# One tile of four banks for the row maxima of windowed attention, scales in a weight tile's corner, and later copies to DRAM

## The chip, the cores and the metric

The kernel runs on one core of a Trainium2 chip. The core has five engines that run side by side and wait for each other by semaphores: TensorE (PE; its weight loads are shown apart as PEld), VectorE (DVE), ScalarE (ACT), GpSimd (POOL) and SyncE (SP), whose queue issues the DMAs here. Matmul results land in PSUM, a memory of eight banks of 512 fp32 columns on 128 partitions, from which VectorE and ScalarE read. The metric is the device time of one execution in microseconds (us).

## What is computed

The input x has 2048 tokens of 512 channels. Cut to what matters:

```python
xn = layernorm(x)
q, k, v = split(xn @ wqkv)                      # 32 heads of 16 channels
scores = q @ k.T * 16 ** -0.5                   # per head
scores = where(0 <= query - key < 256, scores, -1e9)
s = concat(softmax(scores) @ v) @ wo
h = gelu(layernorm(xn) @ w1 + b1)               # 1792 hidden channels
g = silu(h @ w2 + b2)
out = x + s * g
```

## The kernel before

**Split numbers.** fp32 operands go through TensorE as a high and a low part (fp32r), so that a product is three passes: high by high, high by low, low by high.

**Stages.** A start loads x, normalises it and writes its transpose, `big` (the name `xnT` in the profile), with both parts. Then comes attention, then the MLP with its projection `w2` into accumulators `acc`, the product with `wo`, and the gate. Weights and parts of `big` are parked in DRAM and fetched back later (`stage_in`, `keep_xt`, `fetch`).

**Attention by slots.** Heads go in eight groups n of four (a head is one of the places p, a of a pair of pairs). q and k of a group lie in `slots[n % 2]` (tile `qk`); row 3 of each 32 rows of q holds the negated row maximum, which comes in through DRAM (`mT_d`) by way of `max_rows`. There are 128 slots t: slot t stands for block `t % 16` of 128 queries of group `t // 16`. The loop runs over pairs u, of an even slot 2u and an odd slot 2u + 1; pairs with `u % 8 == 0` begin a group of heads. In each pair:

- `prob_part(u, 0..2)` computes transposed scores into the PSUM tile `stb`, ScalarE takes the exponential into `pt`, GpSimd cuts the triangles.
- `pv_part(u)` multiplies `pt` with v into `otb`, which is columns 256 to 511 of the second bank of the PSUM tile `zo`; ScalarE copies it to `oraw` (two buffers) and a DMA takes it to DRAM.
- The row maxima of block t + 12 (`LEAD`) are computed, 12 slots ahead of use.
- Fill units from lists keyed by slot (`fills`) keep TensorE busy: the projections to q, k and v and the first hidden columns, in the banks `fb`. A unit is two matmuls of 64 rows side by side. `plan` and `ends` hold other steps by slot, DMA issues among them; `late` moves some of VectorE's operations to the end of the odd slot.

All instructions of an engine keep the order in which the code issues them.

**The maxima.** A block of 128 queries sees three blocks of 128 keys: the one two before it, partly, the one before it, wholly, and its own, partly. The first and the own are exclusive by position, so `COPY_PREDICATED` with a triangle mask merges the first into the own in PSUM. Two matmuls (a = 1, 0) use the upper and the lower 64 rows of the array and run together: a pair.

- `max_ends` (tile `xy`, two banks): two pairs of 256 columns, first and own keys. Then the merge, and a maximum over 512 elements.
- `max_middle` (columns 0 to 255 of the two banks of `zo`): two pairs of 128 columns and a maximum over 512 elements into a second half of `mt`.
- `max_rows`, every fourth block, joins both halves with a minimum (they are negated) before it sends the rows off.

In an even slot the order is ends, middle, then the operations of VectorE: merge, maximum of the middle, maximum of the ends. In an odd slot the middle comes right behind `prob_part(u, 2)`, then two thirds of the slot's fill units (rounded up), then the ends, the rest of the units, `prob_part(u + 1, 0)` and `pv_part(u)`.

**The scales.** The second layernorm is a scale per token. Its row for the first 512 tokens is spread over the partitions by a DMA (`fetch_scales(0, ...)`): once at slot 80 into a tile with the tag `wa`, which `g_first` takes over at the end of attention, and once more into a tile `scales` after attention. The hidden column tile f = 1 (`first_h(1, False)`) is copied unscaled and multiplied by GpSimd when the second copy is there.

**Copies to DRAM.** `keep_xt` sends twelve pieces of `big` of 512 KB to `xt_d`, behind slots 25, 29, ... 69. `stage_in` copies weights from slot 23 on, one in four slots.

Of the kernel before, what the change touches and what calls it, by code (L numbers as in the profile page):

```python
# [9 lines left out]
F32 = mybir.dt.float32  # L10
# [3 lines left out]
ALU = mybir.AluOpType  # L14
AX = mybir.AxisListType
# [34 lines left out]
def mixer_kernel(ctx, tc, x, wqk, wv, wo, w1, b1, w2, b2, out):  # L50
# [127 lines left out]
    mT_d = dram.tile([NQ, NCH, 32, P], F32, name="mT_d")  # L178


    xy = psum.tile([P, 2, 512], F32, name="xy")
    zo = psum.tile([P, 2, 512], F32, name="zo")
    otb = zo[:, 1, 256:512]
    mids = zo[:, :, 0:256].rearrange("q a (p k) -> q a p k", p=2)
    ends_of = xy.rearrange("q a (p e k) -> q a p e k", p=2, e=2)
    psf = attn.enter_context(tc.tile_pool(name="psf", bufs=1, space=PSUM))
    fb = [psf.tile([P, 512], F32, name=f"fb{i}") for i in range(2)]
    early = ExitStack()
# [33 lines left out]
    nc.gpsimd.memset(mhalf, -0.5)  # L222
    make_identity(nc, ident)
    clear_rows(0, ((nc.vector, 0, 1536), (nc.scalar, 4096, 7168), (nc.gpsimd, 1536, 4096), (nc.gpsimd, 7168, 8192)))
    scales = None
    mask = upper.bitcast(I32).unsqueeze(1).unsqueeze(1).to_broadcast([P, 2, 2, P])
    b1s = const.tile([P, NF], F32, name="b1s")
    sv = small.tile([P, 32], F32, tag="sv", name="sv", bufs=1)
# [258 lines left out]
    def pair_h(f):  # L487

        def mm(ps, k, r, **flags):
            kt, (a, b) = k // 3, PASSES[k % 3]  # L490
            return nc.tensor.matmul(ps, w1_part(a, f)[r, P * kt: P * (kt + 1)], mlp["yy"][b][kt][r], **flags)

        def finish(ps, t, copy):
            raw = t2.tile([P, 512], F32, tag="t2", name=f"hr_{f}")
            if 5 < f < 12:
                copy(raw, ps)
            else:
                nc.vector.tensor_mul(raw, ps, scales)
            if f < 4:
                soon[f] = raw  # L500
            else:
                behind(t, nc.sync.dma_start, h_d[f - 6], raw)
        return 3 * KT, mm, finish
# [51 lines left out]
        r = slice(64 * a, 64 * a + 64)  # L555
        nc.tensor.matmul(out, slot[r, 0, p, P * qb: P * (qb + 1)], keys(slot[r, 1, p]), start=True, stop=True)

    def max_places(n, qb):

        if (n, qb // 4) not in mts:  # L560
            mts[n, qb // 4] = small.tile([P, 2, 2, 2, 4], F32, tag="mt", name=f"mt_{n}_{qb}", bufs=2)
        return (mts[n, qb // 4][:, i, :, :, qb % 4] for i in range(2))

    def max_ends(n, qb):

        mt, _ = max_places(n, qb)
        for p in range(2):
            for a in (1, 0):
                if qb < 2:
                    max_scores(ends_of[:, a, p, 0], n, qb, a, p, lambda row: row[:, P * qb: P * qb + 1].to_broadcast([64, P]))  # L570
                    max_scores(ends_of[:, a, p, 1], n, qb, a, p, lambda row: row[:, P * qb: P * (qb + 1)])
                else:
                    max_scores(ends_of[:, a, p], n, qb, a, p,
                               lambda row: row.rearrange("d (b k) -> d b k", k=P)[:, qb - 2: qb + 1: 2])
        own = ends_of[:, :, :, 1]
        outs["max"] = nc.vector.copy_predicated(own, mask, ends_of[:, :, :, 0]),
        return lambda: nc.vector.tensor_reduce(out=mt, in_=own, axis=AX.X, op=ALU.max, negate=True)

    def max_middle(n, qb):

        if qb == 0:
            return
        _, mu = max_places(n, qb)
        for p in range(2):
            for a in (1, 0):
                max_scores(mids[:, a, p], n, qb, a, p, lambda row: row[:, P * (qb - 1): P * qb])
        nc.vector.tensor_reduce(out=mu, in_=mids, axis=AX.X, op=ALU.max, negate=True)

    def max_block(n, qb):

        rest = max_ends(n, qb)
        max_middle(n, qb)
        rest()

    def max_rows(n, c, t):

        both = mts.pop((n, c))
        mt = both[:, 0]
        mh = small.tile([P, 2, 2, 2, 4], F32R, tag="mh", name=f"mh_{n}_{c}", bufs=2)
        pairs = slice(0 if c else 1, 4)  # L600
        nc.vector.tensor_tensor(mt[:, :, :, pairs], mt[:, :, :, pairs], both[:, 1, :, :, pairs], op=ALU.min)
        eng = nc.gpsimd if t >= -1 else nc.vector
        eng.tensor_copy(mh[:, :, 0], mt)
        eng.tensor_tensor(mh[:, :, 1], mt, mh[:, :, 0].bitcast(F32), op=ALU.subtract)
        mT = small.tile([P, 32], F32, tag="mT", name=f"mT_{n}_{c}", bufs=2)

        for fn, args in todo_dve:
            fn(*args)
        todo_dve.clear()
        nc.vector.transpose(mT, mh.rearrange("p a l i b -> p (a l i b)").bitcast(F32))  # L610
        rows = mT_d[n, c]

        def bring_in():
            nc.sync.dma_start(slots[n % 2][3:P:32, 0, :, 512 * c: 512 * (c + 1)].bitcast(F32),
                              rows.rearrange("(h p b) t -> h p (b t)", h=4, p=2))
        (at if t < 0 else behind)(t + (t < 0), nc.sync.dma_start, rows.rearrange("r (i t) -> i r t", i=4), mT)
        behind(t + 1 + (t < 0), bring_in)
# [67 lines left out]
    def scale_parts():  # L685

        def variance():
            nc.gpsimd.memset(sv, 0.0)
            for i in range(4 * NCH):
                if i in squared:  # L690
                    nc.gpsimd.tensor_scalar(sv[:, i: i + 1], sums[:, i, 1:2], 1.0 / D, None, op0=ALU.mult)
            i = 0
            while i < 4 * NCH:
                k = i
                while k < 4 * NCH and k not in squared:
                    k += 1
                if k > i:
                    nc.gpsimd.tensor_copy(sv[:, i: k], mvs[:, i: k, 1])
                i = k + 1

        def ratio():
            for _ in range(2):
                nc.gpsimd.tensor_tensor(sv[:, 0: 4 * NCH], sv[:, 0: 4 * NCH], rss[:, 0: 4 * NCH], op=ALU.mult)
            nc.gpsimd.tensor_scalar(sv[:, 0: 4 * NCH], sv[:, 0: 4 * NCH], EPS, None, op0=ALU.add)

        def power(c):
            at = sv[:, 4 * c: 4 * c + 4]
            nc.gpsimd.tensor_tensor(at, at, mhalf, op=ALU.pow)
        return variance, ratio, power

    def fetch_scales(c, dst):

# [163 lines left out]
    at(72, nc.vector.transpose, svT, sv)  # L876
    for b in range(4):
        behind(73 + b, nc.sync.dma_start, s_d[:, b], svT[32 * b: 32 * b + 4 * NCH])
    def open_scales():
        nonlocal scales  # L880
        scales = bigp.tile([P, 512], F32, tag="wa", name="scales_0")
        fetch_scales(0, scales)
    behind(80, open_scales)
    for k in range(KT * (NCH - 1)):
        behind(25 + 4 * k, keep_xt, 1 + k // KT, k % KT)
    by_vector = nc.vector.tensor_copy
    on_pool = nc.gpsimd
    for k, (kind, j) in enumerate([*(("w1", j) for j in range(7)), *(("w2", j) for j in range(7)), ("wo", 0), ("wo", 1)]):
# [6 lines left out]
    for f, t, lo_at, lo_by in ((6, 90, 93, nc.vector), (7, 95, 96, nc.vector), (8, 96, 98, on_pool), (9, 99, 101, nc.vector),  # L895
# [4 lines left out]
        at(t, settle, "w1", f, nc.scalar.copy)  # L900
        at(lo_at, settle, "w1", f, None, lo_by)
    at(113, open_w2, 0)
    for f in range(W2_FIRST):
        at(114 + f // 2, fetch, "w2", f)
        at(121 + f, settle, "w2", f, by_vector, nc.vector)
# [8 lines left out]
            split(t[:, 2 * k], t[:, 2 * k + 1], soon[f], by_vector)  # L914
            ready[f] = t[:, 2 * k], t[:, 2 * k + 1]

    def first_h(f, scaled=True):

        for k in range(3 * KT):
            hidden_mm(fb[f], f, k)  # L920
        ready[f] = t2.tile([P, 512], F32, tag="t2", name=f"hf_{f}")
        if scaled:
            nc.vector.tensor_mul(ready[f], fb[f], scales)
        else:
            nc.vector.tensor_copy(ready[f], fb[f])

    ready = {}
    fills[16 * NQ, 0] = [(first_h, (0,))]
# [27 lines left out]

    end = 16 * NQ

    def own_max(part, m):
        return part(m // 16, m % 16) if m < end else lambda: None  # L960

    def own_rows(m, t):
        if 0 <= m < end and m % 4 == 3:
# [24 lines left out]
    for u in range(end // 2):  # L988
        t = 2 * u
        prob_part(u, 1)  # L990
        rest = own_max(max_ends, t + LEAD)
        own_max(max_middle, t + LEAD)
        rest()
        calm[0] = t < end - LEAD
        planned(t)
        fill_in(t, 0)
# [1 line left out]
        ended(t)  # L998
        t += 1
        prob_part(u, 2)  # L1000
        own_max(max_middle, t + LEAD)
        todo = fills.get((t, 0), [])
        n = sum(fn.__name__ == "unit" for fn, _ in todo)
        now[:] = t, 0
        run(delayed.pop((t, 0), ()))
        n -= n if u % 8 == 0 else n // 3
        for fn, args in todo[:n]:
            fn(*args)
        planned(t)
        fill_in(t, 1)  # L1010
        own_max(max_ends, t + LEAD)()
        calm[0] = False
        own_rows(t + LEAD, t)
        for fn, args in todo_dve:
# [15 lines left out]
    for k in sorted(delayed):  # L1030
        run(delayed[k])
    nc.sync.on = False
    first_h(1, False)


    open_w2(1)
# [7 lines left out]
    cp = ctx.enter_context(tc.tile_pool(name="cp", bufs=1))  # L1044
    b2s = cp.tile([P, 512], F32, name="b2s")
    scales = cp.tile([P, 512], F32, name="scales")
    fetch_scales(0, scales)
    wos = cp.tile([P, 2, 4, 512], F32R, name="wos")
    for f in range(W2_FIRST, NF):
        fetch("w2", f)  # L1050
# [4 lines left out]
                              oT_d[2 * g: 2 * g + 2, :, DH].rearrange("i j (c t) -> (i j) c t", c=NCH))  # L1055
        return den

    nc.gpsimd.tensor_tensor(ready[1], ready[1], scales, op=ALU.mult)
    for f in range(6, NF, 2):
        t = gp.tile([P, 2, 512], F32, tag="ohl", name=f"hr_{f}", bufs=4)  # L1060
        nc.sync.dma_start(t, h_d[f - 6: f - 4].rearrange("f p t -> p f t"))
        ready.update({f: t[:, 0], f + 1: t[:, 1]})
        for k in range(2 if f < 12 else 0):
            nc.gpsimd.tensor_tensor(t[:, k], t[:, k], scales, op=ALU.mult)
        if f == 8:
            den = fetch_sums()
    nc.sync.dma_start(b2s, bass.AP(tensor=b2.tensor, offset=b2.offset, ap=[[0, P], [1, 512]]))

    for g in range(4):
# [442 lines left out]
```

## Time and profile before

| | |
|---|---|
| time, median of 3 runs (lowest to highest) | 739.04 us (738.04 to 739.04) |
| time of the profiled execution | 737.41 us |
| its span, first to last instruction | 735.7 us |
| granted TensorE clock, mean over the span | 0.998 |
| attention's main loop (first pv group to the end of the last) | from 67.8 to about 417 us |
| mean DMA rate over the span | 145 GB/s |

Rows of the profile name an instruction by engine, operation, and output<-inputs under the program's tile names: `zo<-pt,vt` is `pv_part`, `zo<-qk` is `max_middle`, `xy<-qk` is `max_ends`, `stb<-qk` is `prob_part`, `fb<-...` are fill units, and `mt<-xy` and `mt<-zo` are the maxima. All have the line L42, that of the helper which keeps the order. In the timeline a row is a run of like instructions: start, length, and in brackets the idle time of the engine before it and what ended it. Matmuls are pipelined: a run's length holds the drain of its last one, while the next run has begun.

### The profile page before, as it was taken

What the parts mean: (1) busy time and instruction counts of PE and PEld (TensorE: products, weight loads), DVE (VectorE), ACT (ScalarE), POOL (GpSimd) and SP (SyncE); (2) the same over time, 40 slices, a digit from 0 to 9 for tenths busy, and PEclk for the clock granted to TensorE, in tenths of its full rate; (3) what the DMA queues carried; (4) which work ended last, traced back from release to release, by engine and by line L of the source; (5) the groups of instructions that cost most, each with busy time, mean ns of one, the idle gap of its engine ahead of it and who ended that gap; (6) DMA issues with size and microseconds to landing.
All of it is one profiled execution on the core that took longest, in us unless ns stands there. A gap on an engine that the chain in (4) does not pass through costs nothing.

```text
span 735.7 us, 17763 instructions
## 1 busy us (share of the span) xinstructions
PE 717.6 (98%) x6944; PEld 580.7 (79%) x6944; DVE 507.7 (69%) x863; ACT 411.7 (56%) x628; POOL 298.9 (41%) x500
## 2 busy tenths in 40 slices
PE   8999999998899999999999999999999999999997
PEld 7998777776678887777777787888888888888886
DVE  7886787876677667778884667536687855667823
ACT  7767777766577566777877726232353734541001
POOL 7344666755468554676777550113202000001102
PEclk9999999999999999999999999999999999999999
DMA  8325455767787733667824465547213322163701
GB/s 294 79 48 126 96 137 142 201 179 205 200 236 202 207 113 97 160 157 192 222 75 153 154 219 147 195 130 238 91 58 104 104 79 86 63 186 113 253 16 58
DMA packets 66275, 106.95 MB, mean 145 GB/s; under 512 B 12624, under 2 KB 21072, under 8 KB 66192
## 3 DMA queue, kind: packets, MB, share of 16 engines
q1 hardware_dynamic: 66192, 105.82, 50.5%
q8 instruction: 55, 0.90, 0.5%
q14 instruction: 28, 0.23, 0.1%
HBM read 54.80 MB, written 33.82 MB: 120 GB/s over the span
## 4 chain that ended last, share of the span: by engine, by line
PE 90%; ACT 3%; DMA 3%; DVE 2%; issue 1%; SPq 0%; POOL 0%; ACTq 0%; DVEq 0%
PE acc L42 20%; PE fb L42 19%; PE zo L42 15%; PE p L42 9%; PE stb L42 7%; PE s L42 6%; PE h L42 6%; PE xy L42 5%; ACT pt L42 2%; PE pv L42 2%; DMA oT_d<-oraw 2%; DMA qk<-sh 1%; DVE mt L42 1%; DMA x<-in_x_dram 1%; SPq L42 0%
## 5 line engine op out<-in xcount | busy, mean ns | idle before, releaser
L42 ACT ACTIVATE pt<-stb 128x1024 f32<-128x1024 f32 (+1 forms) x176 | 177.7, 1009 | 51.7 <-PE stb L42 47.4
L42 POOL TENSOR_SCALAR_AFFINE_SELECT pt<-pt 128x512 f32<-128x512 f32 (+1 forms) x296 | 162.7, 569 | 86.7 <-ACT pt L42 85.8
L42 DVE COPY_PREDICATED xy<-upper,xy 128x512 f32<-128x512 int32 x128 | 88.9, 695 | 61.8 <-PE xy L42 61.6
L42 POOL TENSOR_TENSOR xo<-xo,gated 128x512 f32<-128x512 f32 x15 | 19.9, 1329 | 220.1 <-DVE gated L42 219.1
L42 PE MATMUL fb<-xnT,wqb 64*128 64x512 f32 (+2 forms) x732 | 105.9, 393 | 0.2 <-DVE xy L42 0.2
L42 PE MATMUL acc<-w,gh 128*128 128x512 f32 x320 | 98.7, 390 | 1.5 <-ACT gh L42 1.5
L42 PE MATMUL zo<-pt,vt 128*17 128x128 f32 (+1 forms) x1920 | 90.5, 327 | 0.0
L42 DVE TENSOR_REDUCE mt<-xy 128x4 f32<-128x512 f32 x128 | 88.0, 688 | 2.3
L42 DVE TENSOR_REDUCE mt<-zo 128x4 f32<-128x512 f32 x120 | 82.7, 689 | 6.9 <-PE zo L42 6.4
L42 PE MATMUL stb<-qk 64*128 64x384 f32 (+1 forms) x704 | 76.7, 296 | 2.1 <-ACT pt L42 2.1
L42 PEld LDWEIGHTS stb<-qk 64*128 64x128 f32 x704 | 58.9, 186 | 23.1 <-ACT pt L42 9.4
L42 PEld LDWEIGHTS zo<-pt,vt 128*17 128x17 f32 x1920 | 48.9, 97 | 33.3 <-issue 1.8
L42 PEld LDWEIGHTS acc<-w,gh 128*128 128x128 f32 x320 | 60.0, 188 | 14.3 <-ACT gh L42 1.9
L42 PEld LDWEIGHTS fb<-xnT,wqb 64*128 64x128 f32 (+1 forms) x732 | 61.8, 188 | 6.4 <-DVE xy L42 0.4
L42 PE MATMUL xy<-qk 64*128 64x256 f32 (+2 forms) x608 | 62.2, 291 | 1.1 <-DVE mt L42 1.1
L42 PE MATMUL acc<-w,gl 128*128 128x512 f32 x160 | 62.5, 391 | 0.0
L42 PEld LDWEIGHTS xy<-qk 64*128 64x128 f32 x608 | 48.6, 187 | 8.3 <-DVE mt L42 2.3
L42 PE MATMUL zo<-qk 64*128 64x128 f32 x480 | 48.8, 281 | 6.1 <-ACT oraw L42 5.4
L42 PE MATMUL p<-xnT 128*128 128x512 f32 x189 | 51.8, 389 | 0.0
L42 PEld LDWEIGHTS zo<-qk 64*128 64x128 f32 x480 | 36.3, 186 | 16.0 <-ACT oraw L42 6.9
L42 PE MATMUL s<-wos,ohl 128*128 128x512 f32 (+1 forms) x204 | 44.3, 377 | 0.0
L42 ACT ACTIVATE gated<-acc 128x512 f32<-128x512 f32 x16 | 8.7, 595 | 61.9 <-DVE acc L42 61.9
(210 smaller groups left out, 1212.4 us busy)
## 6 DMA issues: line engine op xcount, KB each, us to landing
qk<-sh SPq DMA_DIRECT2D x128, 128.0 KB
qk<-pjr SPq DMA_DIRECT2D x64, 128.0 KB
oT_d<-oraw SPq DMA_DIRECT2D x64, 128.0 KB
w_d<-in_w_dram SPq DMA_DIRECT2D x14, 512.0 KB
xt_d<-xnT SPq DMA_DIRECT2D x12, 512.0 KB
x<-in_x_dram SPq DMA_DIRECT2D x16, 256.0 KB
w<-w_d SPq DMA_DIRECT2D x16, 256.0 KB
or<-oT_d SPq DMA_DIRECT2D x16, 256.0 KB
```

What stands on the lines that cost most here:

```text
L42: r = issue(*args, **kwargs)
```

## The change

- `xy` and `zo` become one tile `xz` of four banks; `xy` and `zo` are views of it. The maxima of a block are three pairs: place p = 0 as one pair of 384 columns (three key blocks) in banks 0 and 1, place p = 1 as a pair of 128 columns (first keys) behind it and a pair of 256 columns (middle and own) in banks 2 and 3. One merge and one maximum over 1024 elements follow. Blocks 0 and 1 of a group have other pairs. `otb` stays where it was, in what is now the last bank.
- The whole block, `max_block`, stands where the ends stood. In an odd slot one half of the fill units (rounded up) stand ahead of it, not two thirds. The minimum in `max_rows` goes.
- The scales of the first 512 tokens go to a corner of the tile `w2` (columns 7168 to 7679 of its first half, tag `qk0`), fetched at slot 114. `first_h(1)` multiplies by them at once, GpSimd's products of `hr` use them too, and the tile `scales` is fetched behind the DMAs of the sums.
- `keep_xt` goes behind slots 56, 58, ... 78.

```diff
-    xy = psum.tile([P, 2, 512], F32, name="xy")
-    zo = psum.tile([P, 2, 512], F32, name="zo")
+    xz = psum.tile([P, 4, 512], F32, name="xz")
+    xy, zo = xz[:, 0:2], xz[:, 2:4]
     otb = zo[:, 1, 256:512]
...
+    def blocks(at_, step, wide=P):
+
+        v = xz[:, 0, at_: at_ + wide]
+        return bass.AP(tensor=v.tensor, offset=v.offset, ap=[v.ap[0], [512, 2], [step, 2], [1, wide]])
+
+    firsts, own, seen_by = blocks(0, 384), blocks(256, 896), blocks(128, 896, 256)
...
+    def max_block(n, qb):
...
+            mts[n, qb // 4] = small.tile([P, 2, 2, 4], F32, tag="mt", name=f"mt_{n}_{qb}", bufs=2)
+
+        def some(bank, at_, a, p, first, last):
+            keys = slice(P * (qb + first), P * (qb + last))
+            max_scores(xz[:, bank + a, at_: at_ + P * (last - first)], n, qb, a, p, lambda row: row[:, keys])
         for p in range(2):
...
+            elif p == 0:
+                for a in (1, 0):
+                    some(0, 0, a, p, -2, 1)
+            else:
+                for a in (1, 0):
+                    some(0, 384, a, p, -2, -1)
+                for a in (1, 0):
+                    some(2, 0, a, p, -1, 1)
+        outs["max"] = nc.vector.copy_predicated(own, mask, firsts),
+        nc.vector.tensor_reduce(out=mts[n, qb // 4][:, :, :, qb % 4], in_=seen_by if qb else own, axis=AX.X,
+                                op=ALU.max, negate=True)
...
-        nc.vector.tensor_tensor(mt[:, :, :, pairs], mt[:, :, :, pairs], both[:, 1, :, :, pairs], op=ALU.min)
...
+    def first_scales():
+        return mlp["w2", 0][:, 7168:7680].bitcast(F32)
...
-    behind(80, open_scales)
     for k in range(KT * (NCH - 1)):
-        behind(25 + 4 * k, keep_xt, 1 + k // KT, k % KT)
+        behind(56 + 2 * k, keep_xt, 1 + k // KT, k % KT)
...
     at(113, open_w2, 0)
+    at(114, lambda: fetch_scales(0, first_scales()))
...
         prob_part(u, 1)
-        rest = own_max(max_ends, t + LEAD)
-        own_max(max_middle, t + LEAD)
-        rest()
+        own_max(t + LEAD)
...
         prob_part(u, 2)
-        own_max(max_middle, t + LEAD)
...
-        n -= n if u % 8 == 0 else n // 3
+        n -= n if u % 8 == 0 else n // 2
...
-        own_max(max_ends, t + LEAD)()
+        own_max(t + LEAD)
...
-    first_h(1, False)
+    first_h(1)
...
-    fetch_scales(0, scales)
...
-    nc.gpsimd.tensor_tensor(ready[1], ready[1], scales, op=ALU.mult)
...
-            nc.gpsimd.tensor_tensor(t[:, k], t[:, k], scales, op=ALU.mult)
+            nc.gpsimd.tensor_tensor(t[:, k], t[:, k], first_scales(), op=ALU.mult)
         if f == 8:
             den = fetch_sums()
+            fetch_scales(0, scales)
```

More of the change, by code (lines that the diff above doesn't have):

```diff
@@ L178, in mixer_kernel @@
     mT_d = dram.tile([NQ, NCH, 32, P], F32, name="mT_d")
-    xy = psum.tile([P, 2, 512], F32, name="xy")
-    zo = psum.tile([P, 2, 512], F32, name="zo")
+    xz = psum.tile([P, 4, 512], F32, name="xz")
+    xy, zo = xz[:, 0:2], xz[:, 2:4]
     otb = zo[:, 1, 256:512]
-    mids = zo[:, :, 0:256].rearrange("q a (p k) -> q a p k", p=2)
-    ends_of = xy.rearrange("q a (p e k) -> q a p e k", p=2, e=2)
+    def blocks(at_, step, wide=P):
+        v = xz[:, 0, at_: at_ + wide]
+        return bass.AP(tensor=v.tensor, offset=v.offset, ap=[v.ap[0], [512, 2], [step, 2], [1, wide]])
+    firsts, own, seen_by = blocks(0, 384), blocks(256, 896), blocks(128, 896, 256)
     psf = attn.enter_context(tc.tile_pool(name="psf", bufs=1, space=PSUM))
@@ L224, in mixer_kernel @@
     clear_rows(0, ((nc.vector, 0, 1536), (nc.scalar, 4096, 7168), (nc.gpsimd, 1536, 4096), (nc.gpsimd, 7168, 8192)))
-    scales = None
     mask = upper.bitcast(I32).unsqueeze(1).unsqueeze(1).to_broadcast([P, 2, 2, P])
@@ L497, in finish @@
             else:
-                nc.vector.tensor_mul(raw, ps, scales)
+                nc.vector.tensor_mul(raw, ps, first_scales())
             if f < 4:
@@ L556, in max_scores @@
         nc.tensor.matmul(out, slot[r, 0, p, P * qb: P * (qb + 1)], keys(slot[r, 1, p]), start=True, stop=True)
-    def max_places(n, qb):
+    def max_block(n, qb):
         if (n, qb // 4) not in mts:
[L561 to L566, printed above, removed]
+            mts[n, qb // 4] = small.tile([P, 2, 2, 4], F32, tag="mt", name=f"mt_{n}_{qb}", bufs=2)
+        def some(bank, at_, a, p, first, last):
+            keys = slice(P * (qb + first), P * (qb + last))
+            max_scores(xz[:, bank + a, at_: at_ + P * (last - first)], n, qb, a, p, lambda row: row[:, keys])
@@ L567, in max_ends @@
         for p in range(2):
[L568 to L587, printed above, removed]
@@ L589, in max_block @@
-    def max_block(n, qb):
-        rest = max_ends(n, qb)
-        max_middle(n, qb)
-        rest()
+            if qb < 2:
+                for a in (1, 0):
+                    max_scores(xz[:, a, 384 * p: 384 * p + P], n, qb, a, p,
+                               lambda row: row[:, P * qb: P * qb + 1].to_broadcast([64, P]))
+                for a in (1, 0):
+                    some(2 * p, (256 - 128 * p) - P * qb, a, p, -qb, 1)
+            elif p == 0:
+                for a in (1, 0):
+                    some(0, 0, a, p, -2, 1)
+            else:
+                for a in (1, 0):
+                    some(0, 384, a, p, -2, -1)
+                for a in (1, 0):
+                    some(2, 0, a, p, -1, 1)
@@ L595, in max_rows @@
+        outs["max"] = nc.vector.copy_predicated(own, mask, firsts),
+        nc.vector.tensor_reduce(out=mts[n, qb // 4][:, :, :, qb % 4], in_=seen_by if qb else own, axis=AX.X,
+                                op=ALU.max, negate=True)
     def max_rows(n, c, t):
-        both = mts.pop((n, c))
-        mt = both[:, 0]
+        mt = mts.pop((n, c))
         mh = small.tile([P, 2, 2, 2, 4], F32R, tag="mh", name=f"mh_{n}_{c}", bufs=2)
-        pairs = slice(0 if c else 1, 4)
-        nc.vector.tensor_tensor(mt[:, :, :, pairs], mt[:, :, :, pairs], both[:, 1, :, :, pairs], op=ALU.min)
@@ L878, in mixer_kernel @@
         behind(73 + b, nc.sync.dma_start, s_d[:, b], svT[32 * b: 32 * b + 4 * NCH])
-    def open_scales():
-        nonlocal scales
-        scales = bigp.tile([P, 512], F32, tag="wa", name="scales_0")
-        fetch_scales(0, scales)
-    behind(80, open_scales)
     for k in range(KT * (NCH - 1)):
-        behind(25 + 4 * k, keep_xt, 1 + k // KT, k % KT)
+        behind(56 + 2 * k, keep_xt, 1 + k // KT, k % KT)
     by_vector = nc.vector.tensor_copy
@@ L915, in activate_first, with first_h @@
             ready[f] = t[:, 2 * k], t[:, 2 * k + 1]
-    def first_h(f, scaled=True):
+    def first_h(f):
         for k in range(3 * KT):
@@ L921, in first_h @@
         ready[f] = t2.tile([P, 512], F32, tag="t2", name=f"hf_{f}")
[L922 to L925, printed above, removed]
+        nc.vector.tensor_mul(ready[f], fb[f], first_scales())
     ready = {}
@@ L957, in mixer_kernel, with own_max @@
     end = 16 * NQ
-    def own_max(part, m):
-        return part(m // 16, m % 16) if m < end else lambda: None
+    def own_max(m):
+        if m < end:
+            max_block(m // 16, m % 16)
     def own_rows(m, t):
@@ L990, in mixer_kernel @@
         prob_part(u, 1)
-        rest = own_max(max_ends, t + LEAD)
-        own_max(max_middle, t + LEAD)
-        rest()
+        own_max(t + LEAD)
         calm[0] = t < end - LEAD
@@ L1046, in mixer_kernel @@
     scales = cp.tile([P, 512], F32, name="scales")
-    fetch_scales(0, scales)
     wos = cp.tile([P, 2, 4, 512], F32R, name="wos")
```

## The prediction

> **What bounds the kernel now.** First the page: the engines' totals, and their shares of the chain that ended last.
>
> ```profile
> PE 717.6 (98%) x6944; PEld 580.7 (79%) x6944; DVE 507.7 (69%) x863; ACT 411.7 (56%) x628; POOL 298.9 (41%) x500
> PE 90%; ACT 3%; DMA 3%; DVE 2%; issue 1%; SPq 0%; POOL 0%; ACTq 0%; DVEq 0%
> ```
>
> TensorE is the bound: a change gains what it takes off TensorE's queue and loses what it makes that queue wait. The change sits in the attention stage, so next comes the timeline of an ordinary pair of slots there (columns: start us, length us, engine, operation, output and inputs, count).
>
> ```profile
> 314.27 1.50 PE L42 MATMUL zo<-pt,vt 128*17 128x256 f32 x32
> 315.69 0.50 PE L42 MATMUL stb<-qk 64*128 64x384 f32 x4
> 316.03 0.45 PE L42 MATMUL xy<-qk 64*128 64x256 f32 x4
> 316.32 0.38 PE L42 MATMUL zo<-qk 64*128 64x128 f32 x4
> 316.53 1.15 PE L42 MATMUL fb<-xnT,wqb 64*128 64x512 f32 x8
> 317.51 0.40 PE L42 MATMUL stb<-qk 64*128 64x256 f32 x4
> 317.91 0.44 PE L42 MATMUL zo<-qk 64*128 64x128 f32 x4
> 318.18 0.92 PE L42 MATMUL fb<-xnT,wqb 64*128 64x512 f32 x6
> 318.94 0.40 PE L42 MATMUL xy<-qk 64*128 64x256 f32 x4
> 319.19 0.40 PE L42 MATMUL fb<-xnT,wqb 64*128 64x512 f32 x2
> 319.42 0.40 PE L42 MATMUL stb<-qk 64*128 64x384 f32 x4
> 319.75 0.41 PE L42 MATMUL zo<-pt,vt 128*17 128x256 f32 x4
> ```
>
> Matmuls overlap, so a group costs the time to the next group's start. From one pv group (zo<-pt,vt) to the next is 5.48 us: pv 1.42, scores 0.34, ends 0.29, middle 0.21, four fill units 0.98, scores 0.40, middle 0.27, three units 0.76, ends 0.25, one unit 0.23, scores 0.33. There is no hole. The same stretch on VectorE and, of ScalarE, the copy of pv's result:
>
> ```profile
> 313.91 0.70 DVE L42 COPY_PREDICATED xy<-upper,xy 128x512 f32<-128x512 int32 x1 [0.29 <-PE xy L42]
> 314.64 0.69 DVE L42 TENSOR_REDUCE mt<-xy 128x4 f32<-128x512 f32 x1
> 316.52 0.69 DVE L42 COPY_PREDICATED xy<-upper,xy 128x512 f32<-128x512 int32 x1 [0.17 <-PE xy L42]
> 317.16 0.69 DVE L42 TENSOR_REDUCE mt<-zo 128x4 f32<-128x512 f32 x1
> 317.77 0.68 DVE L42 TENSOR_REDUCE mt<-xy 128x4 f32<-128x512 f32 x1
> 318.39 0.69 DVE L42 TENSOR_REDUCE mt<-zo 128x4 f32<-128x512 f32 x1
> 319.39 0.70 DVE L42 COPY_PREDICATED xy<-upper,xy 128x512 f32<-128x512 int32 x1 [0.31 <-PE xy L42]
> 315.83 0.37 ACT L42 COPY oraw<-zo 128x256 f32<-128x256 f32 x1 [0.42 <-PE zo L42]
> ```
>
> VectorE is nearly full, and the order of the work hides it: in the odd slot the middle (bank zo) is done early and the ends (bank xy) late, so zo's maximum is over at 319.08, long before pv writes zo again at 319.75; the maximum of xy, still to come at that time, stands in pv's way nowhere.
>
> The places where TensorE does stand still in this stage, and the sum of them from the view of waits (us, times, longest):
>
> ```profile
> 194.69 0.37 ACT L42 COPY oraw<-zo 128x256 f32<-128x256 f32 x1 [2.25 <-DMA oT_d<-oraw]
> 195.11 0.44 PE L42 MATMUL zo<-qk 64*128 64x128 f32 x4 [1.44 <-ACT oraw L42]
> PE zo L42 <- ACT oraw L42: 5.4, 4, 1.8
> ```
>
> These rows say two things. Copies to DRAM hold up oraw's DMA, and so TensorE, for 5.4 us. And the middle, which writes columns 0 to 255 of zo, waits for a copy that reads columns 256 to 511 of it: waits go by whole banks, not by columns.
>
> **The change part by part.** *Three pairs and one maximum.* Per block the four pairs of matmuls become three of 384, 128 and 256 columns; the same 768 columns stream. A pair saved is worth about 0.10 (half of a middle, 0.21). On VectorE one mask and one maximum over 1024 elements replace the mask and two maxima over 512, and the joining minimum goes. Groups by shape (busy us, mean ns, idle):
>
> ```profile
> L42 DVE TENSOR_REDUCE mt<-xy 128x4 f32<-128x512 f32 x128 | 88.0, 688 | 2.3
> L42 DVE TENSOR_TENSOR mt<-mt 128x16 f32<-128x16 f32 x24 | 4.2, 176 | 0.8
> L42 PE MATMUL xy<-qk 64*128 64x256 f32 x458 | 50.3, 297 | 1.1 <-DVE mt L42 1.1
> ```
>
> From 16 to 512 elements costs 512 ns, so 1024 elements cost about 0.69 + 0.53 = 1.22 us. No row has that shape; its bounds are two maxima end to end, 1.38, and two as they overlap at 317.16 and 317.77, 1.30, or less by the slope, 1.20. I take 1.22. VectorE thus saves about 0.1 us per block, but it is not the bound.
>
> *What the merged tile makes wait.* This is the term that decides. pv's output lies in the last bank of the new tile, and the one maximum reads all four banks. So pv of a pair, which comes right behind the odd slot's maxima, must wait for that maximum, and the next block's maxima must wait for it too. From the start of a block's last pair to the release: matmul 0.30 (row of 297 ns), 0.04 to the mask (316.48 to 316.52), 0.73 from mask to a maximum that needs its result (313.91 to 314.64), 1.22, and 0.06 until TensorE goes on (317.85 to 317.91): 2.35 us. What TensorE has in its queue meanwhile:
> - even block to odd block: its own last pair 0.11, four units 0.98, scores 0.20 (0.40 less the wait for zo's maximum in it), two units 0.50, since two of the four odd units now stand ahead: 1.79. It idles 0.56.
> - odd block to pv: 0.11, two units 0.47, scores 0.33: 0.91. It idles 1.44. Before, this gap did not exist.
> - pv to the even block's last pair: 1.42 + 0.34 + about 0.29 = 2.05, against 1.50 + 0.06 + 0.37 + 0.05 = 1.98 by way of oraw's copy: no idling.
>
> With 0.30 from the first to the last pair of the odd block the pair lasts 2.05 + 2.35 + 0.30 + 2.35 = 7.05 us instead of 5.48. VectorE's late operations and the transpose lie behind the odd maximum, where it now waits for pv anyway.
>
> The first pv groups of the slots with maxima (first and last), and of two starts of a head group:
>
> ```profile
> 67.82 0.84 PE L42 MATMUL zo<-pt,vt 128*17 128x256 f32 x16
> 111.60 0.84 PE L42 MATMUL zo<-pt,vt 128*17 128x256 f32 x16
> 155.55 0.84 PE L42 MATMUL zo<-pt,vt 128*17 128x256 f32 x16
> 395.17 1.06 PE L42 MATMUL zo<-pt,vt 128*17 128x256 f32 x20
> ```
>
> Eight pairs take 155.55 - 111.60 = 43.95 now. Then: six of 7.05; one with the short pv (16 matmuls) saves 0.65, 6.40; one whose block 0 has a maximum of 512 alone saves 0.53, 6.52: 55.2, or 6.90 each. The 58 pairs from 67.82 to 395.17 took 327.4; then 58 x 6.90 = 400. That is +73.
>
> *Copies begun at slot 56.* Twelve DMAs of 512 KB move from slots 25 to 69 to slots 56 to 78, past the sends of q and k and the weights' staging on SP's queue, two slots apart instead of four. The 5.4 us go, but they are inside the 327.4 that I replaced, so they count nothing more. The later crowd is covered by pairs of 7 us; without that cover up to the same 5.4 comes back.
>
> *Scales in w2's corner.* The broadcast is fetched at slot 114 for a first use at 121, seven slots (19 us at 5.48 a pair) ahead: nothing. After attention one GpSimd product and its wait go, and the reload moves behind the sums' DMAs:
>
> ```profile
> 424.92 0.33 SPq L42 DMA_DIRECT2D scales<-s_d  x1
> 428.95 1.29 POOL L42 TENSOR_TENSOR hf<-hf,scales 128x512 f32<-128x512 f32 x1 [12.96 <-DMA scales<-s_d]
> 436.62 0.68 DVE L42 TENSOR_TENSOR g<-h,scales 128x512 f32<-128x512 f32 x1
> ```
>
> TensorE does not wait for that product, so 0; the reload is wanted at 436.62, and the old one, issued at 424.92, let the product start 4 us later. If it came late, 1 to 3 us by estimate. The minima that go (4.2 us) are VectorE's: 0. Before slot 0 there is no pv: 0.
>
> *The clock.* Idle time may cost more than itself. Windows with TensorE's busy time and granted clock:
>
> ```profile
> 192.70:196.10 3.40, 1.96 (x30) 1.45 (x24) 1.14 (x2) 1.09 (x2) 0.70 (x2) 1.00 0.89 236
> 196.10:199.60 3.50, 3.50 (x22) 2.67 (x20) 1.99 (x4) 0.19 (x1) 0.38 (x1) 0.51 0.27 64
> ```
>
> A stretch of 3.4 us with 42% idle was followed by one at half clock. In the new pair 0.56 idle, 1.2 work and 1.44 idle lie within 3.2 us. A 3.4 us window holds 42% idle at about 1.2 of 7.05 us of positions; with two windows a pair that is 20 drops in 58 pairs, each costing up to 1.7 us of work, less the 0.56 it can fill: about 22 us (none: 0; one in each pair: 64). I take 22.
>
> [...]
>
> *Sum.* The profiled execution took 737.4 (span 735.7), 1.6 under the median of the runs, 739.04. 737.4 + 73 + 22 = 832; on the median 834.
>
> **The rivals.**
> - The chain holds and the clock stays: 739 + 73 = 812. For it: 42% is the only such window here that dropped. Chance 0.35; the forecast with drops, from 820 to 880, has 0.50.
> - pv does not wait, only the next block: the pair is 5.48 - 0.20 (scores' wait) - 0.10 + 0.56 = 5.74, +0.26 x 58 = +15, less 7 of oraw's waits and the clock's drop: 747. Against it: the row at 195.11. 0.08.
> - Faster: between an even block's last pair and the odd block's first, VectorE is done within the 1.79 us of work that TensorE has there, and pv has no wait; from that point a pair is 5.18: 58 x 0.30 = 17 and 7 of oraw's waits go: 715. Against it: mask and maximum alone take 1.95. 0.04. That all of it cancels, within 0.2% (1.5 us, about what this kernel's runs can tell): 0.03.
>
> **How the numbers follow.** Point 834. The maximum at 1.20 or 1.38 moves the sum by -2 or +19; a drop in each pair gives 876, none 812; pieces misjudged by 0.1 a gap move it by 12. Together 795 to 885, which leaves out the three small cases. Faster 0.04, same 0.03, slower 0.93.
>
> **What would show it.** In the timeline of a pair: a group of pv matmuls with 1.0 to 1.5 us idle ahead of it, released by VectorE's mt; the odd block's maxima with about 0.5 idle; 7 us from pv to pv; TensorE's busy share in the stage near 70% and granted clock under 1.00 in part of it; one TENSOR_REDUCE of 1.2 us. No wait for oraw's DMA around 165 to 195. I am wrong if pv starts without that wait, or if VectorE's pair of operations is much shorter than 1.95 us.

## The result, and the profile after

| | before | after |
|---|---|---|
| time, median of 4 runs (lowest to highest) | 738.54 us (736.91 to 739.04) | 860.07 us (858.97 to 862.08) |
| ratio to before, 95% interval | | 1.1653 (1.1621 to 1.1685) |
| span of the profiled execution | 735.7 us | 860.4 us |
| mean granted TensorE clock | 0.998 | 0.974 |

The change costs 16.5%. The forecast was 834 in a range of 795 to 885. First the page of after: the engines' totals, and their shares of the chain that ended last. The chain ends early, at 37%, so it says little here; the totals say that TensorE, busy for 98% of the span before, now stands still for a seventh of it, and that VectorE did not fill up instead.

```profile
PE 741.9 (86%) x6688; PEld 579.9 (67%) x6688; DVE 499.6 (58%) x711; ACT 415.8 (48%) x628; POOL 297.4 (35%) x499
PE 37%; DVE 0%; issue 0%
```

For whom TensorE waits is in the view of waits of after (us in total, times, longest us), once for matmuls and once for weight loads:

```profile
PE xz L42 <- DVE mt L42: 94.1, 94, 1.5
PEld xz L42 <- ACT oraw L42: 15.5, 47, 0.8
```

The same view of before, for matmuls that wait for the maxima:

```profile
PE xy L42 <- DVE mt L42: 1.1, 7, 0.2
```

So 1.1 us of waits for the maxima have become 94. Now an ordinary pair of slots in the timeline of TensorE (start us, length us, count, idle time ahead and what ended it), from one pv group to the next:

```profile
349.58 1.50 PE L42 MATMUL xz<-pt,vt 128*17 128x256 f32 x32 [1.19 <-DVE mt L42]
351.00 0.50 PE L42 MATMUL stb<-qk 64*128 64x384 f32 x4
351.60 0.67 PE L42 MATMUL xz<-qk 64*128 64x384 f32 x6
352.10 1.09 PE L42 MATMUL fb<-xnT,wqb 64*128 64x512 f32 x8
353.03 0.40 PE L42 MATMUL stb<-qk 64*128 64x256 f32 x4
353.27 0.63 PE L42 MATMUL fb<-xnT,wqb 64*128 64x512 f32 x4
354.39 0.67 PE L42 MATMUL xz<-qk 64*128 64x384 f32 x6 [0.49 <-DVE mt L42]
354.90 0.62 PE L42 MATMUL fb<-xnT,wqb 64*128 64x512 f32 x4
355.36 0.40 PE L42 MATMUL stb<-qk 64*128 64x384 f32 x4
357.21 0.41 PE L42 MATMUL xz<-pt,vt 128*17 128x256 f32 x4 [1.45 <-DVE mt L42]
```

The pair lasts 357.21 - 349.58 = 7.63 us. The two holes are the forecast ones, 0.49 ahead of the odd block and 1.45 ahead of pv (forecast 0.56 and 1.44). On VectorE, on ScalarE for pv's copy, and for the weight loads (PEld) of the even block's maxima, the same pair:

```profile
352.38 0.70 DVE L42 COPY_PREDICATED xz<-upper,xz 128x512 f32<-128x512 int32 x1 [2.95 <-PE xz L42]
353.11 1.23 DVE L42 TENSOR_REDUCE mt<-xz 128x4 f32<-128x1024 f32 x1
355.10 0.69 DVE L42 COPY_PREDICATED xz<-upper,xz 128x512 f32<-128x512 int32 x1 [0.77 <-PE xz L42]
355.83 1.23 DVE L42 TENSOR_REDUCE mt<-xz 128x4 f32<-128x1024 f32 x1
351.17 0.37 ACT L42 COPY oraw<-xz 128x256 f32<-128x256 f32 x1 [1.00 <-ACT vt L42]
351.60 0.47 PEld L42 LDWEIGHTS xz<-qk 64*128 64x128 f32 x6 [0.30 <-ACT oraw L42]
```

Each engine now waits for the other. VectorE idles 2.95 us for the even block's matmuls, TensorE idles until the maximum ends (355.83 + 1.23 = 357.06, pv at 357.21), and that pv stands ahead of the next block. The even block's first pair starts at 351.60, right behind oraw's copy, which ends at 351.54 and which its weight loads waited for.

The clock is the second part. A window just ahead of a drop, the window of the drop, and the pv groups of a pair with a drop and one without:

```profile
413.90:417.31 3.41, 1.64 (x22) 1.28 (x26) 2.20 (x3) 2.35 (x4) 0.90 (x3) 1.00 0.01 2
417.31:420.72 3.41, 3.41 (x42) 2.30 (x34) 0.21 (x1) 0.74 (x3) 1.11 (x3) 0.50 0.39 106
409.42 1.50 PE L42 MATMUL xz<-pt,vt 128*17 128x256 f32 x32 [1.44 <-DVE mt L42]
417.05 2.56 PE L42 MATMUL xz<-pt,vt 128*17 128x256 f32 x32 [1.44 <-DVE mt L42]
426.00 1.28 PE L42 MATMUL xz<-pt,vt 128*17 128x256 f32 x24 [1.50 <-DVE mt L42]
```

After 3.41 us in which TensorE was busy for 1.64, the clock stood at 0.50 for the next 3.41, and the pair from 417.05 took 8.95 us instead of 7.63. There are 13 such drops while maxima are computed.

Where the 124.7 us between the two spans lie, by pv groups in the two timelines:

| stretch | before | after | difference |
|---|---|---|---|
| start to the first pv | 67.8 | 67.8 | 0 |
| 57 pairs with maxima | 322.9 | 444.3 | +121.4 |
| last six pairs, without maxima | 25.5 | 31.0 | +5.5 |
| from the last pv on | 319.5 | 317.3 | -2.2 |

The pairs with maxima end here (before, then after); the first pair's maxima stand ahead of the first pv, so 57 lie between, not the 58 that the prediction counted up to 395.17:

```profile
390.75 1.50 PE L42 MATMUL zo<-pt,vt 128*17 128x256 f32 x32
```

```profile
512.08 1.50 PE L42 MATMUL xz<-pt,vt 128*17 128x256 f32 x32 [1.45 <-DVE mt L42]
```

### The profile page after: what moved, and what is told of

Same layout as the page of the kernel before. It is cut to its first block, busy times and chain, and to the rows that moved or that the text cites. A ratio compares the mean times of both kernels' runs of the same rounds, so it can differ in the third digit from the quotient of the medians.

```text
span 860.4 us, 17083 instructions
## 1 busy us (share of the span) xinstructions
PE 741.9 (86%) x6688; PEld 579.9 (67%) x6688; DVE 499.6 (58%) x711; ACT 415.8 (48%) x628; POOL 297.4 (35%) x499
## 5 line engine op out<-in xcount | busy, mean ns | idle before, releaser
L42 DVE COPY_PREDICATED xz<-upper,xz 128x512 f32<-128x512 int32 x128 | 89.0, 696 | 198.9 <-PE xz L42 188.8
L42 PE MATMUL xz<-pt,vt 128*17 128x128 f32 (+1 forms) x1920 | 106.3, 367 | 80.8 <-DVE mt L42 71.4
L42 DVE TENSOR_REDUCE mt<-xz 128x4 f32<-128x1024 f32 (+1 forms) x128 | 152.6, 1192 | 4.4
L42 PEld LDWEIGHTS xz<-pt,vt 128*17 128x17 f32 x1920 | 60.2, 106 | 120.4 <-issue 79.3
L42 PE MATMUL xz<-qk 64*128 64x128 f32 (+2 forms) x832 | 89.9, 322 | 28.9 <-DVE mt L42 22.6
L42 PEld LDWEIGHTS xz<-qk 64*128 64x128 f32 x832 | 65.6, 188 | 60.8 <-DVE mt L42 42.1
L42 ACT COPY oraw<-xz 128x256 f32<-128x256 f32 x64 | 23.8, 372 | 119.8 <-PE xz L42 112.2
L42 PEld LDWEIGHTS s<-wos,ohl 128*128 128x128 f32 x204 | 36.8, 188 | 7.1
L42 PEld LDWEIGHTS p<-xnT 128*128 128x128 f32 x189 | 35.5, 188 | 7.3
L42 PE MATMUL fb<-xnT 64*128 64x512 f32 (+1 forms) x240 | 39.9, 396 | 0.1
```

What stands on the lines that cost most here:

```text
L42: r = issue(*args, **kwargs)
```

## The experiments

Each ran beside the kernel before on the same chip (medians of before 737.4, 737.8 and 738.7). The theory: pv's output and the maxima share one tile, so pv and the next block wait for VectorE's mask and maximum; these waits, and the clock that falls because of them, are the whole loss. The rivals are in the expectations.

**Which part costs.** First the maxima alone, the change without its other two edits:

> Before, with the part on the maxima alone (tile of four banks, one maximum, half of the units ahead); the copies to DRAM begin at slot 25 and the scales are as before. Theory 1: the other two parts count nothing, 857 to 865 us. Rival: the copies' later start saves its 5 to 7 us in the slow kernel too, then this one takes 866 to 872.

Measured 861.24 us, ratio 1.1666 (1.1632 to 1.17), with 13 drops of the clock. The maxima are the whole loss. Then the other two edits, alone and together, on the kernel before:

```diff
# copies_alone
-        behind(25 + 4 * k, keep_xt, 1 + k // KT, k % KT)
+        behind(56 + 2 * k, keep_xt, 1 + k // KT, k % KT)
# scales_alone
-    behind(80, open_scales)
+    at(114, lambda: fetch_scales(0, first_scales()))
...
-    first_h(1, False)
+    first_h(1)
...
-    nc.gpsimd.tensor_tensor(ready[1], ready[1], scales, op=ALU.mult)
```

> Before, with the twelve copies to DRAM begun at slot 56 and nothing else changed. Theory 1 (these copies held up oraw's DMA between 160 and 200 us): the waits of TensorE for oraw (5.4 us) and the drop of the clock (1.7 us) go, 731 to 734 us. Rival (the crowd only moves to slots 56 to 78): 737 to 741, with the same waits between 220 and 290 us.

Measured 733.98 us (730.82 to 736.42), ratio 0.9948 (0.9926 to 0.997). The sixteen pairs that lie between these two groups (kernel before, then copies_alone) show where it comes from:

```profile
155.55 0.84 PE L42 MATMUL zo<-pt,vt 128*17 128x256 f32 x16
251.37 0.84 PE L42 MATMUL zo<-pt,vt 128*17 128x256 f32 x16
```

```profile
154.89 0.84 PE L42 MATMUL zo<-pt,vt 128*17 128x256 f32 x16
244.89 0.84 PE L42 MATMUL zo<-pt,vt 128*17 128x256 f32 x16
PE zo L42 <- ACT oraw L42: 1.2, 2, 0.9
```

95.8 us become 90.0, and the waits for oraw over the whole span fall from 5.4 to 1.2. In this execution the clock did not drop, while most others of copies_alone had a mean clock of 0.994 to 0.997; the span became 5.8 shorter here, the median time 3.8.

> Before, with the scales kept in w2's corner and nothing else changed. Theory 1: nothing of it lay on the path, 736 to 739 us. Rival: the late reload makes the gate of the hidden columns wait, 739 to 743; or the earlier product frees a wait of ScalarE and TensorE at 444 us, 735 to 737.

Measured 735.79 us, ratio 0.9972 (0.9956 to 0.9988): a small gain, not nothing. From the last pv to the end the profiled execution took 317.0 us, against 319.5 before. The wait that is gone is TensorE's for `gh` in the MLP, 1.48 of the 2.5 (where the rest went is not shown), in the timeline of before:

```profile
443.92 0.73 PE L42 MATMUL acc<-w,gh 128*128 128x512 f32 x2 [1.48 <-ACT gh L42]
```

> Before, with the later copies and the scales in w2's corner, the maxima as before. Theory 1: the sum of both alone, 729 to 734 us, faster than before and than the changed kernel.

Measured 728.21 us (728.09 to 729.1), ratio 0.9874 (0.9852 to 0.9895), clock 1.000. This version beats both kernels, by 9.6 us against before, a little more than I expected. In the profiled executions the gains add up (spans shorter by 5.8 and 2.4 alone, by 8.3 together). In the merged kernel the same two edits are worth next to nothing (860.07 against 861.24): a stretch in which the maxima set the pair has no use for oraw's DMA coming sooner.

**Does the maximum lie on the path?** The changed kernel with a maximum over 512 elements, the middle blocks alone, so that it leaves out the own and first keys:

```diff
-    firsts, own, seen_by = blocks(0, 384), blocks(256, 896), blocks(128, 896, 256)
+    firsts, own, seen_by = blocks(0, 384), blocks(256, 896), blocks(128, 896)
```

> The changed kernel, but the one maximum reads 512 of the 1024 elements (the middle keys of both places; the others are left out of the maximum). Theory 1 (the pair is a chain through VectorE): the release comes 0.53 us earlier twice in a pair, so the pair falls from 7.63 to about 6.57, 58 pairs give 61 us, and the gap ahead of pv falls from 1.45 to 0.9; with fewer drops of the clock the run takes 780 to 800 us. Rival (TensorE's own work, by more expensive pairs or the clock, sets the pair): no change, 850 to 862.

Measured 791.23 us, ratio 1.0718 (1.0695 to 1.0742). By shape (busy us, mean ns, idle), and pv of one pair and the next:

```profile
L42 DVE TENSOR_REDUCE mt<-xz 128x4 f32<-128x512 f32 x128 | 88.6, 693 | 4.4
343.37 1.50 PE L42 MATMUL xz<-pt,vt 128*17 128x256 f32 x32 [0.91 <-DVE mt L42]
349.93 0.41 PE L42 MATMUL xz<-pt,vt 128*17 128x256 f32 x4 [0.91 <-DVE mt L42]
```

The maximum is shorter by 1.225 - 0.69 = 0.53 us and the pair by 7.63 - 6.56 = 1.07, twice as much: both maxima of a pair lie wholly on the path. The clock did not drop in its pairs.

**Bank or tile?** Two kernels that compute the maxima for a = 1 alone, so that these need two banks only; the mask has 256 elements, and the maximum reads 1024 (512, each twice). They differ in one thing: whether pv's banks are a tile of their own.

```diff
# apart
+    xy = psum.tile([P, 2, 512], F32, name="xy")
+    zo = psum.tile([P, 2, 512], F32, name="zo")
# shared
+    xz = psum.tile([P, 4, 512], F32, name="xz")
+    xy, zo = xz[:, 0:2], xz[:, 2:4]
```

> The changed kernel, but the maxima are computed for the upper rows (a = 1) alone, in a tile of two banks, and pv's output lies in another tile, as before the change. The maximum still reads 1024 elements (each twice), the merge works on 256; the maxima of the other heads are left out, theirs are copies. Theory 1 (pv waits for the maximum because both lie in one tile): nothing stands ahead of pv, the pair falls from 7.63 to 5.3 to 5.6 us, the whole run takes 720 to 750 us. Rival (the three pairs and the long maximum themselves are the cost, or the falling clock): the pair stays over 6.5 us and the run over 800.

> The kernel with half of the maxima left out as in the one named apart, but its two banks and pv's two banks are one tile of four again, as in the changed kernel. The maxima touch banks 0 and 1 alone, pv's output lies in bank 3. If waits go by whole banks (what the prediction said), pv waits for nothing and the run is as the one named apart, 720 to 750 us. If they go by whole tiles, pv waits for the maximum: the merge is some 0.25 us shorter in each block, so the pair is about 7.1 us and the run 820 to 840.

Apart: 727.81 us, ratio 0.9848 (0.981 to 0.9885), pairs of 5.4 to 5.5. Shared: 818.89, ratio 1.1091 (1.1067 to 1.1115), pairs of 7.08, 1 us under what I expected of whole tiles. The waits of the one, then waits and timeline of the other:

```profile
PE xy L42 <- DVE mt L42: 5.3, 11, 0.6
```

```profile
PE xz L42 <- DVE mt L42: 71.5, 90, 1.2
343.73 1.50 PE L42 MATMUL xz<-pt,vt 128*17 128x256 f32 x32 [1.17 <-DVE mt L42]
```

In both, pv writes one bank and the maxima read two others. Where these are one tile, pv waits 1.17 us for a maximum that never touches its bank, and the kernel takes 91 us longer. The wait belongs to the tile, not to a bank. It does not hang on the hand-made access patterns of the maximum either: in after the even block's first matmuls, plain slices of banks 0 and 1, start 0.05 to 0.11 us behind the end of oraw's copy out of bank 3 in each of the 57 pairs; in before, where they had a tile of their own, they started at least 0.16 us ahead of that end.

**Can order alone cost it?** The kernel before, with the ends early and the middle late in an odd slot, and the even slot's maximum of the ends ahead of the middle's:

```diff
-        own_max(max_middle, t + LEAD)
+        own_max(max_ends, t + LEAD)()
...
-        own_max(max_ends, t + LEAD)()
+        own_max(max_middle, t + LEAD)
```

> Before, with ends and middle exchanged in the odd slot (ends early, middle where the ends stood, and in the even slot the maximum of the ends ahead of that of the middle). No work is added or left out; but the maximum of zo, the tile that pv writes, now comes last. Theory 1: pv starts 0.4 to 0.6 us later in each pair, 58 pairs give 23 to 35 us: 760 to 775 us. Rival (pv does not wait for a maximum in its tile): 737 to 742.

Measured 779.55 us, ratio 1.0568 (1.0546 to 1.0591), above what I expected, with pairs of 6.45:

```profile
239.99 1.50 PE L42 MATMUL zo<-pt,vt 128*17 128x256 f32 x32 [0.82 <-DVE mt L42]
246.44 0.41 PE L42 MATMUL zo<-pt,vt 128*17 128x256 f32 x4 [0.80 <-DVE mt L42]
```

With the same instructions, pv now finds its tile held by the late middle's maximum. So the order of before, middle early and ends late, was worth 42 us, and the change gave it up along with the second tile.

**What does the clock cost?** In the changed kernel, an odd slot has half of its fill units ahead of its maxima. Two kernels put none and all of them there; work and chain stay the same.

```diff
-        n -= n if u % 8 == 0 else n // 2
+        n -= n                              # units_behind
+        n -= n if u % 8 == 0 else 0         # units_ahead
```

> The changed kernel with all fill units of an odd slot behind its maxima (before: half ahead). Theory 1 (VectorE's mask and maximum set the pair; TensorE's order only says where its idle time lies): pairs stay at 7.6 us, idle about 1.0 ahead of the odd maxima and 1.0 ahead of pv instead of 0.5 and 1.45; with the idle time spread there are fewer drops of the clock than 13: 842 to 852 us. Rival (TensorE's own work is part of the chain): the pair changes by 0.3 us or more, below 835 or above 865.

> The changed kernel with all fill units of an odd slot ahead of its maxima. Theory 1 (VectorE's chain sets the pair): pairs stay at 7.6 to 7.7 us, idle near 0 ahead of the odd maxima and about 1.9 ahead of pv; the idle time comes in one lump, so there are as many drops of the clock as before or more (13 to 25): 858 to 880 us. Rival (drops go by the share of idle time and not by its lumps): 13 drops, 860 us. Rival 2 (TensorE's work ahead of the maxima now delays them): pairs over 7.9 us.

Behind: 843.98 us (843.64 to 844.25), ratio 1.1421 (1.1395 to 1.1448), no drop. Ahead: 874.36, ratio 1.1836 (1.1801 to 1.1872), 18 drops. The pair without a drop is 7.63 us in both. A pair of the first, and the longer hole of the second:

```profile
276.83 1.50 PE L42 MATMUL xz<-pt,vt 128*17 128x256 f32 x32 [0.96 <-DVE mt L42]
281.65 0.67 PE L42 MATMUL xz<-qk 64*128 64x384 f32 x6 [0.93 <-DVE mt L42]
284.47 0.59 PE L42 MATMUL xz<-pt,vt 128*17 128x256 f32 x5 [0.96 <-DVE mt L42]
```

```profile
445.00 1.28 PE L42 MATMUL xz<-pt,vt 128*17 128x256 f32 x24 [1.91 <-DVE mt L42]
```

Moving work does not change the pair, since VectorE's chain sets it; it changes how the idle time is lumped, and so the clock. In medians the drops cost 860.07 - 843.98 = 16 us in after and 30 in units_ahead. In the profiled executions, where they can be counted, the 13 cost 17.9 us, 1.4 each, and the 18 cost 29.7, 1.6 each.

**Three pairs with two tiles.** The whole change, but place p = 0 in `xy` and p = 1 in `zo`, p = 1 early in the odd slot and p = 0 late, each with a mask and a maximum of its own, and two thirds of the fill units ahead, as in the kernel before:

```diff
-        own_max(t + LEAD)
+        own_max(t + LEAD, (1,))     # behind prob_part(u, 2)
...
+        own_max(t + LEAD, (0,))     # where the ends stood
```

> Three pairs and the other two edits kept, but xy and zo are tiles of their own again: place p = 0 is reduced in xy, place p = 1 in zo, each with a mask of 256 columns (0.43 us) and a maximum over 512 (0.69), and in the odd slot p = 1 stands early and p = 0 late. Theory 1 (the loss comes from pv waiting for a maximum that shares its tile; the three pairs themselves are good): pv finds zo released, pairs of 5.2 to 5.4 us, 715 to 728 us. Rival (VectorE's chain of a block is the limit whatever the tiles; it is 4.5 us a pair here): pairs of 6 us or more, 760 us or more.

Measured 772.16 us, ratio 1.0455 (1.0428 to 1.0481): my expectation failed and the rival held. One pair:

```profile
343.76 0.33 PE L42 MATMUL xy<-qk 64*128 64x128 f32 x2 [0.20 <-DVE zo L42]
344.49 0.39 PE L42 MATMUL zo<-qk 64*128 64x256 f32 x2 [0.40 <-DVE mt L42]
346.23 0.41 PE L42 MATMUL zo<-pt,vt 128*17 128x256 f32 x4
342.21 0.43 DVE L42 COPY_PREDICATED xy<-upper,xy 128x256 f32<-128x256 int32 x1 [0.55 <-PE xy L42]
343.74 0.69 DVE L42 TENSOR_REDUCE mt<-zo 128x2 f32<-128x512 f32 x1
344.92 0.43 DVE L42 COPY_PREDICATED zo<-upper,xy 128x256 f32<-128x256 int32 x1 [0.48 <-PE zo L42]
```

pv no longer shows a wait. But the even block's two masks and two maxima run end to end from 342.21 to 344.43, and the odd block's early part waits for the last of them; then its own mask must be done before its maximum, where before the early part, the middle, had none. The tiles are not wholly apart either: the first keys of p = 1 lie in `xy`, so the even block's mask on zo, which reads them, holds back the odd block's next matmuls (0.20, the first row). What is left, as these rows suggest, is again a chain between TensorE and VectorE, 6.27 us a pair. What three pairs are worth with no such chain was not shown by any run.

## Why the prediction was right, point by point

*The mechanism* was right: pv, and the next block behind it, wait for the one maximum. The waits, the holes of 0.49 and 1.45 and the runs shared, apart and half_max show it.

*The length of the maximum*, forecast 1.22 from the slope of two shapes, measured 1.225. The smaller shape was that of another operation, a TENSOR_TENSOR, so that its slope fitted was partly luck; the runs themselves give 1.225 - 0.69 = 0.53 for 512 more elements.

*"Waits go by whole banks"* is the step that failed: here they go by whole tiles (pv's 1.17 us in shared). It changed the size, not the sign. I let the even block's first two pairs, in banks 0 and 1, pass ahead of oraw's copy, which reads bank 3, and had only its last pair 2.05 us behind pv. In the trace the first pair is 2.02 behind pv.

*The pair*, forecast 7.05, is 7.63. Of the 0.58, 0.27 is that wait. The rest are the releases: 2.79 from the even block's first pair to the odd block's, and 2.82 on to pv, where the sum had 0.30 + 2.35 = 2.65. The blocks' matmuls hold the mask back for 0.78 (351.60 to 352.38) and 0.71 (354.39 to 355.10) instead of 0.64, and pv follows the maximum after 0.15 instead of 0.06. That the two holes match all the same is partly luck: TensorE's own work between them took longer too, by 0.21 and 0.16. Over 57 pairs 6.90 each was forecast, 393; units_behind, without drops, has 494.22 - 68.06 = 426.2, or 7.48 each:

```profile
68.06 0.84 PE L42 MATMUL xz<-pt,vt 128*17 128x256 f32 x16
494.22 1.49 PE L42 MATMUL xz<-pt,vt 128*17 128x256 f32 x32 [0.99 <-DVE mt L42]
```

*The clock*, forecast 20 drops and 22 us: 13 drops, and 444.3 - 426.2 = 18 us in the profiled executions (16 in the medians). The total came near by luck: there were fewer drops than forecast, at 1.4 us each instead of 1.1. The border taken for them, 42% idle, was too low for this kernel: in after, stretches with 45 to 46% idle (from 103.29, 369.53 and 376.35, busy for 1.86, 1.85 and 1.89 of 3.41 us) kept the clock. The rival in which the clock stays is wrong for this kernel; in units_behind the clock does stay. A stretch without any work was not needed: the window from 413.90 was 48% busy, and the clock fell. The first drops of after begin at 89.6, 113.5, 137.4, 161.3, 185.2 and 215.9, in steps of 23.9 and 30.7, which are 7 and 9 times 3.41, the length of one drop.

*The last six pairs* have no maxima, and their +5.5 was not foreseen; the prediction had 2.5 of it by chance, since it counted the first of them as a pair with maxima (6.90 instead of 4.42). There the scores alternate between `stb` and the banks of `xy`, now in pv's tile, so they wait for oraw's copy, and pv for the exponential. In the timeline of after:

```profile
514.10 0.50 PE L42 MATMUL xz<-qk 64*128 64x384 f32 x4 [0.53 <-ACT oraw L42]
518.20 1.50 PE L42 MATMUL xz<-pt,vt 128*17 128x256 f32 x32 [1.21 <-ACT pt L42]
```

*Copies at 0* was right in the merged kernel, where its cover is the pairs of 7.6 us. *Scales at 0* was off by 2: the stretch behind the last pv is 2.2 shorter in after and 2.5 in scales_alone. The step that failed there is "TensorE does not wait for that product": the wait for `gh` of 1.48 went.

The sum again, on the profiled executions: 832 + 33 (57 pairs) - 4 (clock) + 3 (last six pairs) - 2 (scales) = 862, as measured (862.08). The terms that were missed partly cancel; the pair's is the one that moved the point.

## What to carry to other kernels

Before two results that live side by side are put into one tile, list who writes and who reads each part: with waits placed as in these kernels, the slowest reader of any part then holds back every writer of all parts, here 91 us for parts in separate banks. Fewer, longer instructions on an engine that was not the bound gained nothing here, while they lengthened the time until a buffer is released; what counts is that release, and the order that hides it. When idle time can't be avoided, spread it: the same idle sum in two equal holes instead of a short and a long one was worth 16 us.

## What the runs showed of the hardware

In after, a drop of the clock did not need a stretch without any work. Each of the 13 drops lasted 3.41 us at a granted clock of 0.50, and they began whole multiples of 3.41 us apart. In the 3.41 us ahead of each, TensorE was busy for 41 to 51% (1.39 to 1.72 us, worked out from the trace's matmuls). Of the other stretches in that step the least busy, 1.75 us from 485.58, kept the clock. units_behind, with no drop, had one of 52%:

```profile
348.70:352.10 3.40, 1.77 (x18) 1.45 (x18) 2.60 (x3) 1.68 (x2) 0.71 (x2) 1.00 0.43 159
```

So the two kinds part near a half in these two kernels. Before has no such border: TensorE was busy for 1.97 of 3.41 us ahead of its drop (from 192.73), and for 1.93 in a stretch behind which the clock stayed at 1.00 (from 441.90). What else decides there stays open.
